# Block-decayed attention feeding an ELU MLP on one core: where the decay factors are applied, zero matmuls in the opening, and a new order of all work

## The chip, the cores and the metric

The kernel runs on one core of a Trainium2 chip. The metric is the device time of one execution in microseconds. The kernel before took 221.75 us (median of three runs, 221.27 to 222.61).

Names used below: PE is TensorE (matmuls; PEld its weight loads), DVE is VectorE, ACT is ScalarE, POOL is GpSimd, SP is SyncE. POOL issues the loads from memory (they convert float32 to float16 on the way), SP issues the DMA transposes and the stores of results.

## The reference

```python
B, H, S, D = 4, 8, 768, 64        # batch, heads, sequence, head size; blocks of 64
rel   = pos[:, None] - pos[None, :]
Dmask = where(rel >= 0, lam ** rel, 0)                 # one lam per head
for each block b:                                      # 12 blocks, in order
    intra = (qb @ kb.T * Dmask) @ vb
    inter = (qb * lam ** (pos + 1)) @ kv_state
    out_b = intra + inter
    kv_state = lam ** 64 * kv_state + (kb * lam ** (63 - pos)).T @ vb
x = out as rows of 512 (8 heads x 64), 3072 rows
h = x @ w_in                                           # 512 -> 2048
g = where(h > 0, h, exp(min(h, 0)) - 1)
result = g @ w_out                                     # 2048 -> 512, float32
```

## The kernel before

The kernel works in chunks of 128 positions instead of 64, which is possible because the decay between two positions is a product of a factor of the key and a factor of the query. There are six chunks for each of four batches, and so 24 groups: group g is chunk g // 4 of batch g % 4, with all eight heads in it. Groups g and g + 1 (g even) share one tile of x, 256 rows wide. The kernel writes its whole order by hand: ORDER is a string of tokens, and every token appends instructions to the queues of the engines, which run them strictly in that order. Two steps on different engines wait for each other only through the data and the buffers. The tokens, with what they do:

- `L:k8` loads k for groups 8 and 9 (POOL issues it; groups 0 to 3 are loaded singly, all later ones in pairs, 256 KB as float16). `i:3` and `o:3` load parts of w_in and w_out. q of group 0 alone is loaded as float32 by SP.
- `d:8` (att_kd, L275) multiplies k by its decay factors ks, on POOL (`:p`) or DVE (`:v`), giving kd.
- `t:q4` (L304) transposes q or k of one group on PE, and `e:q4` (att_T_out, L313 to L317) brings the result from PSUM to SBUF. From group 8 on, `D:k8` (att_T_dma, L297) does the same by a DMA transpose that SP issues.
- `s:8` (L328) computes the eight score tiles of a group into two PSUM banks, `E:8:0` and `E:8:1` (L335, DVE) multiply them by the mask and give pp.
- `p:8` (L349, L355) sums pp with v and, from chunk 1 on, q with the state stp, into psO; `x:8` (att_X, L372 to L376) moves psO to x.
- `u:8` (L419) computes the state's increment from kd and v, `y:8` (L402, or L396 in chunk 0; two halves on DVE) adds the old state, and `m:8` (L386, POOL) multiplies by the decay of a chunk, giving the next stp.
- `1:8:5` (L451) computes part 5 of the hidden layer for groups 8 and 9 into psH (two buffers), `h:8:5` (L461, L462, ACT) takes exp and relu, `g:8:5` (L436, DVE) joins them into g. `2:8:1` (L475) adds a quarter of the second matmul of group 8 into psM; the last quarter is followed by an ACT copy (L501) and a store. `R` (L487) does the last 128 columns of group 23.
- `z:1:0` clears a state tile, `qs:1` makes a part of the query factors qs, and `row`, `col`, `ident`, `caus`, `upp`, `ks`, `qn`, `logp` make constants. `w:3` (three matmuls of zeros) exists in the code but stands nowhere in ORDER; ten matmuls of zeros run ahead of it.

Where the decay is applied before: the key's factor is in kd, and kd is what is transposed into kT. The query's factor is applied ahead of the scores in groups 0 to 7 (by `scaled` for group 0, L263, and in the eviction of the transpose for the others, L313) and in the eviction of x from group 8 on (`GPE = 8`, L372). The mask of `E` is then only causal (`causT`, zeros and ones, the same for all heads).

BANKS names the PSUM bank of every tile: of eight banks, two hold psH and six (A, B, C, D, M0, M1) go round among transposes, scores, psO, psU and psM. The DMA transposes read kd, which has eight buffers; kT and qT have six buffers each, and the paired loads have four per tensor.

Of the kernel before, what the change touches and what calls it, by code (L numbers as in the profile page):

```python
# [15 lines left out]
def kernel(  # L16
# [11 lines left out]
    nc = tc.nc  # L28
# [11 lines left out]
    GPE = 8  # L40
# [54 lines left out]
    )  # L95
    BANKS = (
# [111 lines left out]
    qn = cpool.tile([128, H], FP32, name="qn")  # L208
# [16 lines left out]
    def const_qn():  # L225
        nc.scalar.activation(qn[:], loglam[:], AF.Exp, scale=col[:, 0:1])
# [33 lines left out]
    def scaled(w, g, eng):  # L260

        t = asb.tile([128, H, 64], FP16, tag="kd" if w == "k" else "qd", name=f"{w}d{g}", bufs=8 if w == "k" else 4)
        {"v": nc.vector, "p": nc.gpsimd}[eng].tensor_tensor(  # L263
            out=t[:], in0=raw[f"{w}{g}"][:],
            in1=(ks if w == "k" else qn)[:].unsqueeze(2).broadcast_to([128, H, 64]), op=ALU.mult,
        )
        if w == "k":
            kds[g] = t
        else:
            nat["q"][g] = t[:].unsqueeze(1)  # L270
# [23 lines left out]
    def att_T_dma(w, g):  # L294
        t = asb.tile([128, NHP, 128], FP16, tag=f"{w}T", name=f"{w}T{g}", bufs=6)
        src = of("q", g) if w == "q" else kds[g][:]
        nc.sync.dma_start_transpose(out=t[:], in_=src.rearrange("p h d -> p (h d)"))  # L297
        qkT[(w, g)] = t

    def att_T_pe(w, g):  # L300
        pt = bank(f"T{w}{g}", 0, [128, NHP, 128], FP16, f"psT{w}{g}")
        src = of("q", g) if w == "q" else kds[g][:]
        for hp in range(NHP):
            nc.tensor.transpose(  # L304
                pt[:, hp, :], in_=src[:, 2 * hp : 2 * hp + 2, :], identity=ident16[:]
            )
        psT[(w, g)] = pt

    def att_T_out(w, g, eng):
# [4 lines left out]
        elif eng == "v":  # L314
            nc.vector.tensor_copy(t[:], pt[:])
        else:
            nc.scalar.copy(out=t[:], in_=pt[:])  # L317
# [246 lines left out]
```

## Time and profile before

| | |
|---|---|
| median of three runs | 221.75 us |
| profiled execution: its own time | 222.63 us |
| profiled execution: span | 220.9 us, mean granted clock 0.959 |
| busy: PE, DVE, ACT, POOL | 206.0, 133.6, 126.6, 94.4 us |
| last matmul ends, last store lands | 217.6, 219.7 us |
| loads of q, k, v in pairs: issue to landing, median | 10.2 to 10.5 us |
| DMA transposes: issue to landing, median | 4.6 us (q), 4.8 us (k) |

The span runs from the program's first instruction to its last; what lies around it (1.7 us here) is in the execution's own time. PE's busy time is the time in which a matmul was in flight, with ends that are modelled; the clock is what the throttle granted, 1.00 being full speed. A row of the costliest groups gives line, engine, operation, tile written <- tiles read, count, busy time, mean duration of one, and the idle time of that engine just before them with what ended it.

### The profile page before, as it was taken

Reading aid. Unit: us, or ns where it says so; the run is one execution under the profiler, and the core shown is the slowest. Engines: PE = TensorE matmul, PEld = TensorE weight load, DVE = VectorE, ACT = ScalarE, POOL = GpSimd, SP = SyncE. Lnnn points to the kernel's source line nnn. Section 1 sums busy time; section 2 is a strip of 40 time slices with the busy share of each in tenths; the row PEclk is TensorE's granted clock in tenths of the full one; section 3 lists DMA queues with packets and bytes.
Section 4 is the critical chain, followed back from the end, with each engine's and each line's share of the span. In section 5 each row is a group of like instructions: output and inputs, shape, how many; then the busy total and the mean of one; then the engine's idle time right before and its main releaser. Section 6 shows DMA issues by size and latency. Waiting matters only on the chain.

```text
span 220.9 us, 4883 instructions
## 1 busy us (share of the span) xinstructions
PE 206.0 (93%) x1946; PEld 138.8 (63%) x1946; DVE 133.6 (60%) x232; ACT 126.6 (57%) x241; POOL 94.4 (43%) x113
## 2 busy tenths in 40 slices
PE   7489899999995599999999999999999999999994
PEld 2366666775763456776667676666686667676652
DVE  3787687764895457859377835487785544433230
ACT  4545666764664036656746656665665756565353
POOL 7998786968397366285942402002060000000000
PEclk9758999999999679999999999999999999999999
DMA  8999999999999999997999230502017011010115
GB/s 85 155 166 189 185 188 173 196 159 156 190 153 158 156 146 178 163 96 150 128 186 129 65 99 0 142 3 88 34 49 46 3 47 47 3 49 0 50 49 190
DMA packets 101975, 24.57 MB, mean 111 GB/s; under 512 B 92608, under 2 KB 99008, under 8 KB 101952
## 3 DMA queue, kind: packets, MB, share of 16 engines
q0 software_dynamic: 79760, 13.50, 79.3%
q1 hardware_dynamic: 22192, 10.76, 23.3%
q8 instruction: 15, 0.25, 0.4%
q14 instruction: 8, 0.07, 0.1%
HBM read 27.27 MB, written 6.29 MB: 152 GB/s over the span
## 4 chain that ended last, share of the span: by engine, by line
PE 77%; DVE 8%; DMA 5%; ACT 3%; POOL 2%; issue 1%; SPq 1%; ACTq 0%; POOLq 0%
PE psM L475 34%; PE psH L451 33%; DMA qT<-qn 4%; PE psS L328 3%; DVE pp L335 3%; PE psO L349 2%; DVE g L436 2%; PE psO L355 1%; DMA lam_b<-in_lam_dram 1%; DVE stt L402 1%; DVE stp L396 1%; PE psTk L304 1%; PE psU L419 1%; DVE qT L313 1%; POOL kd L275 1%
## 5 line engine op out<-in xcount | busy, mean ns | idle before, releaser
L436 DVE SCALAR_TENSOR_TENSOR g<-e,psH 128x512 f16<-128x512 f32 x96 | 65.7, 685 | 60.1 <-ACT psH L462 58.8
L451 PE MATMUL psH<-xt,wi 128*128 128x256 f16 x768 | 98.0, 276 | 1.4 <-ACT psH L462 1.2
L461 ACT ACTIVATE e<-psH 128x512 f32<-128x512 f32 x96 | 57.2, 596 | 64.5 <-PE psH L451 64.4
L475 PE MATMUL psM<-wo,g 128*128 128x512 f16 (+1 forms) x384 | 93.1, 382 | 0.1
L451 PEld LDWEIGHTS <-wi 128*128 128x128 f16 x768 | 74.1, 99 | 23.1 <-DVE g L436 2.0
L475 PEld LDWEIGHTS <-g 128*128 128x128 f16 x384 | 37.6, 99 | 33.6 <-issue 1.9
L462 ACT ACTIVATE psH<-psH 128x512 f32<-128x512 f32 x96 | 57.1, 595 | 0.0
L386 POOL TENSOR_TENSOR stp<-stt,upp 64x256 f16<-64x256 f32 x32 | 19.5, 609 | 59.1 <-DVE stt L402 49.5
L335 DVE TENSOR_TENSOR pp<-psS,causT 128x512 f16<-128x512 f32 x48 | 31.4, 684 | 10.9 <-PE psS L328 10.6
L501 ACT COPY osb<-psM 128x512 f32<-128x512 f32 x23 | 13.5, 586 | 17.8 <-PE psM L475 17.8
L275 POOL TENSOR_TENSOR kd<-kn,ks 128x512 f16<-128x512 f16 x18 | 18.5, 1043 | 4.1 <-issue 2.9
L159 POOL DMA_DIRECT2D kn<-in_k_dram x14 | 15.6, 1113 | 1.4 <-POOLq L548 0.8
L159 POOL DMA_DIRECT2D vn<-in_v_dram x14 | 15.3, 1096 | 2.1 <-issue 1.9
L159 POOL DMA_DIRECT2D qn<-in_q_dram x13 | 14.6, 1122 | 1.9 <-DMA qn<-in_q_dram 1.9
L328 PE MATMUL psS<-qT,kT 64*128 64x128 f16 x192 | 9.1, 237 | 6.6 <-DMA qT<-qn 4.9
L402 DVE TENSOR_TENSOR stt<-stp,psU 64x256 f32<-64x256 f16 x32 | 13.3, 414 | 0.5
L328 PEld LDWEIGHTS <-kT 64*128 64x128 f16 x192 | 6.5, 103 | 10.9 <-issue 10.2
L349 PE MATMUL psO<-pp,vn 128*64 128x128 f16 x192 | 12.8, 228 | 0.0
L372 DVE TENSOR_TENSOR xt<-psO,qs 128x512 f16<-128x512 f32 x16 | 10.8, 684 | 3.0 <-PE psO L355 2.4
L349 PEld LDWEIGHTS <-vn 128*64 128x64 f16 x192 | 10.0, 114 | 1.5 <-issue 1.4
L355 PE MATMUL psO<-qT,stp 128*64 128x128 f16 x160 | 10.6, 219 | 0.0
L355 PEld LDWEIGHTS <-stp 128*64 128x64 f16 x160 | 9.0, 110 | 0.0
(46 smaller groups left out, 74.9 us busy)
## 6 DMA issues: line engine op xcount, KB each, us to landing
out_dram<-osb SPq DMA_DIRECT2D x23, 256.0 KB, 2.2
qn<-in_q_dram POOLq DMA_DIRECT2D x10, 256.0 KB, 10.4
kn<-in_k_dram POOLq DMA_DIRECT2D x10, 256.0 KB, 10.5
vn<-in_v_dram POOLq DMA_DIRECT2D x10, 256.0 KB, 10.2
wi<-in_moe_w_in_dram POOLq DMA_DIRECT2D x8, 256.0 KB, 8.8
wo<-in_moe_w_out_dram POOLq DMA_DIRECT2D x8, 256.0 KB, 10.4
kn<-in_k_dram POOLq DMA_DIRECT2D x4, 128.0 KB, 4.9
vn<-in_v_dram POOLq DMA_DIRECT2D x4, 128.0 KB, 5.2
```

The costliest lines, as they stand in the source:

```text
L159: nc.gpsimd.dma_start(out=t[:].rearrange("p b h d -> p (b h) d"), in_=src)
L275: {"v": nc.vector, "p": nc.gpsimd}[eng].tensor_tensor(out=kd[:], in0=of("k", g), in1=ks[:].unsqueeze(2).broadcast_to([128, H, 64]), op=ALU ...
L328: nc.tensor.matmul(psS[g][hh][:, hp, :], lhsT=kt[r, hp, :], rhs=qt[r, hp, :], start=True, stop=True,)
L335: nc.vector.tensor_tensor(out=P[:], in0=psS[g][hh][:], in1=causT[:].unsqueeze(1).broadcast_to([128, NHP, 128]), op=ALU.mult,)
L349: nc.tensor.matmul(po[r, hp, :], lhsT=vt[:, 2 * hp + hh, :], rhs=Pt[(g, hh)][:, hp, :], start=True, stop=(cb == 0), skip_group_check=True,)
L355: nc.tensor.matmul(po[r, hp, :], lhsT=stp[b][cb % 2][:, hp, r], rhs=qt[:, hp, :], start=False, stop=True, skip_group_check=True,)
L386: nc.gpsimd.tensor_tensor(out=new[r, :, r], in0=stt.pop((g, hh))[r], in1=upp[r].unsqueeze(2).broadcast_to([64, NHP, 64]), op=ALU.mult,)
L436: nc.vector.scalar_tensor_tensor(out=g[:].rearrange("p f c t -> p (f c t)"), in0=e[:], scalar=-1.0, in1=r[:], op0=ALU.add, op1=ALU.min,)
L451: nc.tensor.matmul(pH[:, f * n * 128 : (f + 1) * n * 128], lhsT=wi16[i][:, kk, w * 128 : (w + 1) * 128], rhs=xg[g0][:, kk, :], start=(kk = ...
L461: nc.scalar.activation(e[:], pH[:], AF.Exp)
L462: nc.scalar.activation(pH[:], pH[:], AF.Relu)
L475: nc.tensor.matmul(psM[g][:, cols], lhsT=gts[(g, j * FB + f)], rhs=wo16[i][:, w, cols], start=first and f == 0, stop=end and f == FB - 1, ...
```

## The change

Keys and queries now go into the transposes as they were loaded, for all groups and on both ways (PE and DMA). The key's factor moves into the mask, which therefore is one tile for each head (`mask`, 128 x 1024 float32, made once on DVE), and the query's factor is applied in the eviction of x for all groups, always on DVE. kd remains for the state's increment and is no longer made for groups 20 to 23, whose state nobody reads. q of group 0 is only cast.

```diff
-    GPE = 8
-    qn = cpool.tile([128, H], FP32, name="qn")
+    mask = cpool.tile([128, H, 128], FP32, name="mask")
...
-    def const_qn():
-        nc.scalar.activation(qn[:], loglam[:], AF.Exp, scale=col[:, 0:1])
+    def const_mask():
+        nc.vector.tensor_tensor(
+            out=mask[:], in0=causT[:].unsqueeze(1).broadcast_to([128, H, 128]),
+            in1=ks[:].unsqueeze(2).broadcast_to([128, H, 128]), op=ALU.mult,
+        )
...
-    def scaled(w, g, eng):
...
+    def cast_raw(w, g, eng):
+        t = asb.tile([128, H, 64], FP16, tag=f"{w}d", name=f"{w}d{g}", bufs=4)
+        if eng == "a":
+            nc.scalar.copy(out=t[:], in_=raw[f"{w}{g}"][:])
...
     def att_T_dma(w, g):
-        src = of("q", g) if w == "q" else kds[g][:]
+        src = of(w, g)
...
     def att_T_pe(w, g):
-        src = of("q", g) if w == "q" else kds[g][:]
+        src = of(w, g)
...
     def att_T_out(w, g, eng):
-        if w == "q" and f"q{g}" not in raw:
-            nc.vector.tensor_tensor(out=t[:], in0=pt[:], in1=qs[:], op=ALU.mult)
-        elif eng == "v":
+        if eng == "v":
...
     def att_E(g, hh):
-            out=P[:], in0=psS[g][hh][:],
-            in1=causT[:].unsqueeze(1).broadcast_to([128, NHP, 128]), op=ALU.mult,
+            out=P[:], in0=psS[g][hh][:], in1=mask[:, hh::2, :], op=ALU.mult,
...
     def att_X(g):
-        if g >= GPE:
-            nc.vector.tensor_tensor(out=dst, in0=po[:], in1=qs[:], op=ALU.mult)
-        elif eng == "v":
-            nc.vector.tensor_copy(dst, po[:])
-        else:
-            nc.scalar.copy(out=dst, in_=po[:])
+        nc.vector.tensor_tensor(out=dst, in0=po[:], in1=qs[:], op=ALU.mult)
```

ORDER and BANKS are new throughout. The new ORDER holds the same steps, but for `qn` (gone), `mask` (new), `d:20` to `d:23` (gone) and four tokens of zero matmuls, `w:3`, `w:5`, `w:1` and `w:2`, eleven matmuls in all. Its opening, the stretch with the first DMA transposes, and its end:

```
L:k0 z:3:0:a L:k1 z:1:1:a i:1 log z:1:0:a iota col L:k2 row ks a:q0:a ident caus logp L:q1 t:q0 mask
upp t:k0 w:3 qs:2 e:q0:a L:v0 e:k0:a t:k1 d:0:v s:0 w:5 L:k3 d:1:v e:k1:v L:v1 E:0:1 L:q3 E:0:0 t:k2
t:q1 d:2:v L:q2 e:q1:a e:k2:v u:0 qs:1 p:0 i:0 s:1 t:k3 w:1 E:1:1 i:3 e:k3:a E:1:0 u:1 qs:0 qs:3
L:q4 p:1 x:0 t:q3 w:2 y:1 e:q3:a L:v2 x:1 s:3 t:q2 L:v3 E:3:1 1:0:1 e:q2:a z:0:1:v z:3:1:a L:k4 y:0
s:2 h:0:1 1:0:0 E:2:0 o:0 E:3:0 h:0:0 o:1 g:0:1 E:2:1 i:2 1:0:3 g:0:0 d:3:p h:0:3 u:2 p:2 t:q5 x:2
i:4 p:3 e:q5:a u:3 x:3 t:q4 o:2 e:q4:a y:3 1:2:0 o:3 g:0:3 t:k4 d:4:p h:2:0 t:k5 e:k4:v 1:2:3 d:5:p
e:k5:a s:4 g:2:0 h:2:3 s:5 E:4:0 i:5 1:2:1 z:2:1:a i:6 g:2:3 2:1:0 h:2:1 y:2 i:7 1:2:2 E:4:1 o:5
2:0:0 g:2:1 h:2:2 L:v4 1:0:2 g:2:2 L:q6 2:3:0 h:0:2 1:2:4
...
D:k8 d:9:v g:4:6 d:8:p 2:0:3 D:k9 s:7 s:6 E:7:0 1:4:7 D:q12 E:6:0 1:4:1 h:4:7 E:6:1 E:7:1 u:6 u:4
p:6 h:4:1 y:4 D:k11 p:7 m:4 g:4:7 u:7 u:5 2:3:3 y:5 D:k10 m:5 1:4:2 g:4:1 x:6 1:4:0 D:q11 h:4:2
d:10:p x:7 2:4:2 L:v10 h:4:0 g:4:2 D:q10 s:8 s:9 E:8:0 1:6:6 L:k14 g:4:0 2:4:3 h:6:6 E:8:1 D:k13
d:12:p y:7 1:4:3 g:6:6 d:13:p 2:4:0 h:4:3 D:k12 E:9:0 1:6:3 E:9:1 m:7 g:4:3 u:8 h:6:3 p:9 y:6 L:k16
u:9 p:8 y:9 s:11 D:q13 2:4:1 L:q18 E:11:0 g:6:3 1:6:5 E:11:1 1:6:2 x:8 h:6:5 2:5:1 x:9 h:6:2 g:6:5
2:5:3 z:2:0:a 1:8:4 g:6:2 m:6 d:11:v 1:6:1 h:8:4 L:v14 s:12 s:10 h:6:1 E:12:1 2:5:0
...
2:15:2 1:22:7 h:22:6 2:22:1 2:23:2 h:22:7 g:22:6 2:20:3 g:22:7 1:20:5 2:23:3 h:20:5 2:22:3 g:20:5 R
1:18:3 1:18:1 h:18:3 2:22:0 h:18:1 g:18:3 2:19:3 2:22:2 g:18:1 1:18:2 1:20:4 h:18:2 2:19:0 h:20:4
g:18:2 2:18:2 2:19:1 g:20:4 2:20:2 2:18:1 2:18:0 2:21:2
```

Before, the corresponding stretch around the DMA transposes read:

```
D:k8 E:7:1 1:4:0 E:6:0 L:k18 1:4:3 D:k9 h:4:0 E:7:0 E:6:1 u:4 L:q14 u:6 p:7 h:4:3 y:4 p:6
g:4:0 u:7 d:12:p u:5 2:2:3 y:5 m:5 D:k12 1:4:2 g:4:3 x:6:a 1:4:6 h:4:2 d:11:p x:7:v 2:3:3 d:10:p
D:k11 g:4:2 s:9 s:8 y:6 1:6:6 L:v10 h:4:6 D:k10 E:8:0 2:4:1 E:9:1 h:6:6 m:4 D:q10 g:4:6 2:4:0 g:6:6
L:q12 1:6:0 D:q11 E:9:0 1:4:4 d:13:p y:7 h:6:0 E:8:1 u:8 p:9 m:7 D:k13 h:4:4 g:6:0 u:9 p:8 1:6:5 x:8
L:k16 g:4:4 2:4:3 h:6:5 x:9 s:11 s:10
```

More of the change, by code (lines that the diff above doesn't have):

```diff
@@ L258 @@
     kds, qkT, Pt, psS, psT, psO, psU, psUU, xg = {}, {}, {}, {}, {}, {}, {}, {}, {}
-    def scaled(w, g, eng):
[L262 to L268, printed above, removed]
-        else:
-            nat["q"][g] = t[:].unsqueeze(1)
+    def cast_raw(w, g, eng):
+        t = asb.tile([128, H, 64], FP16, tag=f"{w}d", name=f"{w}d{g}", bufs=4)
+        if eng == "a":
+            nc.scalar.copy(out=t[:], in_=raw[f"{w}{g}"][:])
+        else:
+            {"v": nc.vector, "p": nc.gpsimd}[eng].tensor_copy(t[:], raw[f"{w}{g}"][:])
+        nat[w][g] = t[:].unsqueeze(1)
     def att_kd(g, eng="p"):
@@ L359, in att_P, with att_X @@
         psO[g] = po
-    def att_X(g, eng="a"):
+    def att_X(g):
         po = psO.pop(g)
@@ L507 @@
         "iota": emit_iota, "col": const_col, "row": const_row, "log": const_log,
-        "qn": const_qn, "ks": const_ks, "ident": const_ident, "caus": const_caus,
+        "mask": const_mask, "ks": const_ks, "ident": const_ident, "caus": const_caus,
         "logp": const_logp, "upp": const_upp,
@@ L519, in run @@
             x, g = a[0][0], int(a[0][1:])
-            {"L": emit_load, "a": scaled, "t": att_T_pe, "e": att_T_out}[w](x, g, *a[1:])
+            {"L": emit_load, "a": cast_raw, "t": att_T_pe, "e": att_T_out}[w](x, g, *a[1:])
         elif w == "D":
```

104 rows, old and new, of tables (BANKS, ORDER) are left out of this document.

## The prediction

> **What bounds the kernel now.** I read the page first, for the busy share and clock along the span, then three windows, PE's timeline around the hole they show, the chain of waits back from it, and SP's own waits.
>
> The page, second part (one digit is 5.5 us):
> ```profile
> PE   7489899999995599999999999999999999999994
> PEclk9758999999999679999999999999999999999999
> DMA  8999999999999999997999230502017011010115
> ```
> PE is full except in the opening and in slices 12 and 13, and both stretches have a low clock too. The DMA engines are full for the first 100 us. The windows put numbers on it (busy us of PE, PEld, DVE, ACT, POOL; then clock, DMA):
> ```profile
> 30.00:69.00 39.00, 38.86 (x438) 27.07 (x435) 29.51 (x52) 25.32 (x49) 30.02 (x32) 1.00 1.90 174
> 69.00:80.00 11.00, 6.14 (x33) 3.21 (x33) 4.77 (x9) 1.90 (x4) 4.24 (x6) 0.69 2.08 144
> 80.00:217.00 137.00, 136.84 (x1254) 92.68 (x1253) 78.81 (x131) 82.64 (x155) 33.59 (x41) 1.00 0.58 79
> ```
> From 30 to 69 and from 80 to 217 nothing but PE's own work can shorten the kernel. PE's timeline in between:
> ```profile
> 68.14 1.03 PE L475 MATMUL psM<-wo,g 128*128 128x512 f16 x4
> 74.02 1.03 PE L328 MATMUL psS<-qT,kT 64*128 64x128 f16 x16 [4.86 <-DMA qT<-qn]
> 74.99 1.89 PE L451 MATMUL psH<-xt,wi 128*128 128x256 f16 x8
> 76.67 3.49 PE L475 MATMUL psM<-wo,g 128*128 128x512 f16 x8
> ```
> s:11 waits for a DMA transpose. Four psM take 0.86 us of PE (1.73 for eight in the chain), so PE is free at 69.0 and idles 5.0 us. Then sixteen psS, eight psH and eight psM last from 74.02 to 80.17, 6.15 us, where the chain elsewhere has 0.55 + 0.87 + 1.73 = 3.15 us: 3.0 us go to a halved clock. The hole costs **8.0 us**. The chain tells why the transpose was late:
> ```profile
> 59.75 2.04 POOL kd L275 x2
> 61.80 1.16 POOL vn L159
> 62.97 0.64 POOL stp L386
> 63.61 0.44 SPq L297
> 64.14 1.32 SPq L297
> 65.51 8.37 DMA qT<-qn
> ```
> SP issues in order. D:k10 waits for kd10 on POOL, D:q10 and D:q11 stand behind it, and then the transfer needs 8.37 us in the full queue. SP's own waits (us in total, times, longest) say that it is a pattern:
> ```profile
> SPq L297 <- POOL kd L275: 19.5, 6, 5.6
> SPq L297 <- DVE stt L402: 9.3, 1, 9.3
> ```
>
> **The change, part by part.** Both programs hold the same matmuls but for eleven more zeros (w:3, w:5, w:1, w:2), so I count the time that PE loses besides its work.
>
> *Plain k into the DMA transposes.* D:k8 to D:k13 no longer wait for kd. In the new order D:q8 follows its load alone. The trace's landings give the price of a full queue: a 256 KB load every 1.67 us (48.27, 49.94, 51.60). From 47.28 to 73.89 it finished nine loads (15.0 us), nine transposes and three stores, so the latter twelve took 11.6 us, about 1.0 us each. In the new order qn8 is the 31st load; the 32nd landed at 44.36 before, so about 43.2. Up to q11 there follow two weights (1.3 each, by the landings 40.52, 41.84, 43.09), five loads, eight transposes, three stores: 10.9 + 8.2 + 2.2 = 21.3 us, hence 64.5 at best. But q11 is issued only when qn10 has landed, about 60, and issue to landing took 6.6 to 8.5 us in that stretch: 66.6 to 68.5. PE reaches s:11 after 51.7 us of work (steps of 0.87 for eight psH, 0.86 for four psM, 0.28 for eight psS), with 15.7 us lost (15.4 in the opening, below, and 0.3 in small gaps): 67.4. Idle there 0 to 1.1 us instead of 5.0. D:k13 and D:k12 wait for kn12 (about 67): k12 lands at 73 to 78, taken 75.5, and PE comes to s:12 about 74. Idle 0 to 4, taken 1.4. Later ones are due when the queue has eased: k14, behind qn16 and qn14, which POOL issues only after the state product of group 8, lands at 95 to 97, and s:14 comes at about 97: 0 to 1, taken 0. kd10 and the other kd now stand behind stp products on POOL; u:10, the first user, comes 15 us after kd10, so that costs nothing, and if POOL were that late u:10 would wait for it.
>
> *All x, and the earlier y and E, on DVE.* Between u:6 and 1:8:5 the new order gives DVE 14 E (0.684 us, L335), 20 halves of y (0.414, L402), 16 g (0.685, L436), 6 x (0.684, L372), one kd (0.683): 33.6 us, against 31 to 32 us of PE steps in the same stretch. Before, such a stretch of 24 us of PE work held 23.5 us of DVE. So DVE becomes a bound for some 32 us: up to 2.6 us, though a PE that waits for a transpose lets DVE catch up. Together with the two idles above I put **+3.0 us** (0 to 6) where 8.0 stood. A gap under 1.5 us has not dropped the clock in this trace: 1.18 us of idle at 21.7 left it at 1.00.
>
> *The opening.* Gone: q's decay and the seven qT evictions on DVE (0.676 each; now ACT copies of 0.56 to 0.59, some DVE copies of 0.42). New: the mask on DVE, 1024 wide. No row shows it; two 512-wide products (2 x 0.683) bound it above, one below; it is nearest to two, so 1.3. Walk of DVE: loglam_p done 5.8, mask 7.0, kd0 and kd1 8.4, kT1 8.8, two E 10.0, kd2 and kT2 11.1; then s:1, behind p:0 and vn0 (landed 11.01), gives E:1 at 12.2 to 13.5; x:0 waits for the last qs on ACT (13.8), then x:0, y:1, x:1 (2.2 us) to 16.0. So 1:0:1 starts at 16.1, before at 16.37. From there to g:2:2 DVE has 13.4 us in a row and waits 0.8: 30.2, and PE starts 1:2:4 at 31.05 having done 16.0 us of work. Before, 1:2:4 started at 31.72 after 16.1. The walk has the clock full; were it half until 18.5, s:1, 1:0:1 and s:2 add about 0.9. So 15.05 us lost against 15.6; the walk leaves out small gaps, and I take 15.4, **-0.2 us** (-0.6 to +1.2). The granted clock was 0.58 from 10 to 20 us although PE was busy 8.39 of 10. [...]
>
> *The end.* R moves ahead of the last psM, so the last eviction is 128x512 (0.586, was 0.266) and the last store lands in 2.0 us, not 1.76: **+0.55 us**. The dropped kd20 to kd23 cost nothing before (POOL idled 49.5 us beside them). A kn buffer is now held until its transposes land; kn16, the first load to need such a buffer, is due only at about 67, ten us after they do.
>
> Sum: span 220.9 - 8.0 + 3.0 - 0.2 + 0.55 = 216.3. The profiled execution took 222.63, 1.73 more than its span: 218.0. It lay 0.9 above the median of 221.75, so **217.1 us**. The likeliest case's own range is 215 to 219.
>
> **Rivals.** *No hole at all*: queue and DVE keep up, residue 0: 214.1. For it: the queue's bare work ends at 64.5. Against: 33.6 us of DVE.
> *One idle long enough to halve the clock*: k12 lands at 77 or later; 3 us more, as after 74.02: 220.1. For it: kT13 took 8.19 us before.
> *Slower*: the clock drops twice, at s:11 and at s:12, because loads and transposes share the queue: each time 2 us of idle and 3 us of half clock, 10 us for the 3.0: 224.1. It decides from idles of about 1.8 us each: the clock here changes at steps of 3.41 us (4.81, 8.22, 18.46, 73.08, 79.91), it stayed full with 1.18 us of idle, and it fell at 8.22 after a step in which PE worked about half the time. For it: the DMA column is nearly as high from 30 to 69 (1.90) as in the hole (2.08). Against: SP would have to issue q11 2 us later than I have it.
> [...]
>
> **How the numbers follow.** Forecast 0.50 (0.15 of it with the half clock in the opening), no hole 0.18, one dropped clock 0.19, two 0.13. The range 213.9 to 222.0 leaves out the double drop and the best edge. 0.5% (1.1 us), about what a measurement can tell, puts the limits at 220.6 and 222.9: faster 0.50 + 0.18 + 0.11 = 0.79, same 0.09, slower 0.12.
>
> **What would show it.** Right: PE's digits near 9 in slices 11 to 14; SP's waits on POOL's kd gone; no wait of psS for a DMA over 2 us; DVE near 10 of 10 from 56 to 88; PE's last matmul at about 212.5. Wrong: a psS wait of over 3 us with PEclk below 1 behind it, or 1:2:4 later than 33.

## The result, and the profile after

The changed kernel takes 226.97 us (median of four runs, 225.91 to 228.12), beside 221.99 us for the kernel before: a ratio of 1.0239 with a 95% interval of 1.0206 to 1.0272. It is 2.4% slower where 2% faster was forecast. Here and below, ratios leave out executions more than 1.5% above the fastest of their kernel, while medians and ranges hold all of them. Its profiled execution took 225.91 us with a span of 224.1 us and a mean clock of 0.977, against 222.63, 220.9 and 0.959 before.

The second part of the page of the changed kernel:

```profile
PE   7787999999997999954999999999999999999992
PEclk9969999999999999996799999999999999999999
DMA  8999999999999999999999675010120001101114
```

Counted from 0, the hole of slices 12 and 13 is gone but for a 7 in slice 12. There is a new one in slices 17 and 18, and it too has a low clock at its end (slices 18 and 19). The windows of the changed kernel size both (busy us of PE, PEld, DVE, ACT, POOL; then clock, DMA):

```profile
60.00:69.50 9.50, 7.87 (x108) 5.51 (x106) 8.14 (x16) 5.09 (x10) 4.28 (x5) 1.00 1.78 159
69.50:98.00 28.50, 27.89 (x296) 19.54 (x296) 21.94 (x38) 16.43 (x32) 24.20 (x29) 1.00 1.75 140
98.00:109.00 11.00, 4.93 (x32) 2.72 (x31) 2.57 (x4) 2.17 (x5) 4.64 (x5) 0.69 2.09 186
```

The last line is nearly a copy of the line from 69 to 80 us of the kernel before (clock 0.69, DMA 2.08): the hole has not been closed but moved 29 us later. PE's timeline of the changed kernel shows who waits there; the bracket is the idle time ahead and what ended it:

```profile
69.50 0.40 PE L324 MATMUL psS<-qT,kT 64*128 64x128 f16 x8 [1.63 <-DMA qT<-qn]
...
104.18 1.04 PE L324 MATMUL psS<-qT,kT 64*128 64x128 f16 x16 [6.07 <-DMA kT<-kn]
105.15 1.89 PE L465 MATMUL psM<-wo,g 128*128 128x512 f16 x4
106.83 1.91 PE L441 MATMUL psH<-xt,wi 128*128 128x256 f16 x8
108.54 2.07 PE L465 MATMUL psM<-wo,g 128*128 128x512 f16 x8
110.45 1.04 PE L441 MATMUL psH<-xt,wi 128*128 128x256 f16 x8
```

s:11 waits 1.6 us, s:12 (76.02) not at all, and s:14 waits 6.1 us for the transpose of k14. Behind it eight psH take 1.91 us where they take 1.04 at 110.45, which is the halved clock (granted 0.50 from 102.04 to 108.87). The chain of waits leads one step further back:

```profile
94.82 1.29 SPq L295
...
96.20 7.93 DMA kT<-kn
104.14 0.05 issue
104.18 1.04 PE psS L324 x16
```

k14 was issued late, at 96.2 us, and then took 7.9 us. SP's row and POOL's row of the same stretch stand side by side in the changed kernel:

```profile
89.60 2.50 SPq L295 DMA_TRANSPOSE qT<-qn  x2
92.19 1.22 SPq L295 DMA_TRANSPOSE kT<-kn  x1
93.52 2.59 SPq L295 DMA_TRANSPOSE qT<-qn  x2
96.20 2.72 SPq L295 DMA_TRANSPOSE kT<-kn  x2
```
```profile
93.61 1.21 POOL L158 DMA_DIRECT2D vn<-in_v_dram  x1
94.81 1.17 POOL L158 DMA_DIRECT2D kn<-in_k_dram  x1
95.95 1.17 POOL L158 DMA_DIRECT2D vn<-in_v_dram  x1
97.08 1.18 POOL L158 DMA_DIRECT2D qn<-in_q_dram  x1
```

SP's row q16, q17, k17, q15, q14, k14 starts when qn16 lands (89.55), and every transpose takes SP 1.3 us. POOL issues four loads at the same time (v22, k18, v18, q20, for groups of which the first, s:18, is due on PE at 133.8 us): v22 stands 1.2 us ahead of q14, three of the four ahead of k14, and q20 0.9 us behind it. The trace's landings: k17, issued at 92.19, took 2.51 us, q14 6.97 and k14 7.93. The balance of the span (+3.2 us): the hole at s:11 gone -8.0, s:11 now +1.8, a gap inside p:12 +0.9, s:14 with its halved clock +8.5, the end +0.6, and -0.6 in the opening and small gaps.

### The profile page after: what moved, and what is told of

The parts are those of the page before. It is cut to its first block, busy times and chain, and to the rows that moved or that the text cites. A ratio compares the mean times of both kernels' runs of the same rounds, so it can differ in the third digit from the quotient of the medians.

```text
span 224.1 us, 4888 instructions
## 1 busy us (share of the span) xinstructions
PE 207.3 (92%) x1957; PEld 138.2 (62%) x1957; DVE 133.9 (60%) x231; ACT 128.1 (57%) x243; POOL 89.5 (40%) x108
## 4 chain that ended last, share of the span: by engine, by line
PE 78%; DMA 9%; DVE 5%; POOL 2%; issue 2%; ACT 1%; SPq 1%; POOLq 0%; ACTq 0%
PE psH L441 35%; PE psM L465 34%; DMA kT<-kn 4%; DMA qT<-qn 3%; PE psS L324 3%; PE psO L344 2%; DMA vn<-in_v_dram 2%; DVE pp L331 2%; PE psO L350 2%; DVE g L426 1%; POOL kn L158 1%; PE psU L409 1%; SPq L295 1%; DVE xt L366 1%; ACT e L451 1%
## 5 line engine op out<-in xcount | busy, mean ns | idle before, releaser
L465 PE MATMUL psM<-wo,g 128*128 128x512 f16 (+1 forms) x384 | 93.6, 380 | 0.0
L331 DVE TENSOR_TENSOR pp<-psS,mask 128x512 f16<-128x512 f32 x48 | 31.6, 685 | 13.0 <-PE psS L324 12.7
L273 POOL TENSOR_TENSOR kd<-kn,ks 128x512 f16<-128x512 f16 x13 | 13.4, 1038 | 12.8 <-DMA kn<-in_k_dram 8.6
L366 DVE TENSOR_TENSOR xt<-psO,qs 128x512 f16<-128x512 f32 x24 | 16.1, 686 | 1.9 <-PE psO L350 0.9
L324 PEld LDWEIGHTS <-kT 64*128 64x128 f16 x192 | 6.0, 99 | 12.1 <-DMA kT<-kn 6.6
L120 PE MATMUL psZ<-zero 128*128 128x512 f16 x21 | 8.0, 528 | 1.2 <-DVE zero L115 1.2
```

What stands on the lines that cost most here:

```text
L324: nc.tensor.matmul(psS[g][hh][:, hp, :], lhsT=kt[r, hp, :], rhs=qt[r, hp, :], start=True, stop=True,)
L331: nc.vector.tensor_tensor(out=P[:], in0=psS[g][hh][:], in1=mask[:, hh::2, :], op=ALU.mult,)
L366: nc.vector.tensor_tensor(out=dst, in0=po[:], in1=qs[:], op=ALU.mult)
L465: nc.tensor.matmul(psM[g][:, cols], lhsT=gts[(g, j * FB + f)], rhs=wo16[i][:, w, cols], start=first and f == 0, stop=end and f == FB - 1, ...
```

## The experiments

The theory: the change did close the hole it aimed at, and the new order opened another, because q14 and k14 are issued (a) late and (b) among four loads that nobody needs yet. The rivals: (a) alone, (b) alone, DVE as the bound, and the move of the decay itself. Ratios are against the kernel before on the same chip.

**The four loads held back (e1).** A copy on POOL that reads the masked scores of group 17 stands ahead of them:

```diff
+    def gate(g, hh):
+        nc.gpsimd.tensor_copy(gate_sb[:], Pt[(g, hh)][:, 0, 0:8])
 ORDER
-  1:8:7 L:v22 h:8:2 D:k15 2:6:1 L:k18 h:8:7 g:8:2 2:7:1 L:v18 1:8:0 g:8:7 1:8:3 L:q20 h:8:0 s:14
-  s:17 d:16:p h:8:3 g:8:0 2:6:3 E:17:1
+  1:8:7 h:8:2 D:k15 2:6:1 h:8:7 g:8:2 2:7:1 1:8:0 g:8:7 1:8:3 h:8:0 s:14
+  s:17 d:16:p h:8:3 g:8:0 2:6:3 E:17:1 G:17:1 L:k18 L:v22 L:v18 L:q20
```

> The changed kernel with the four loads v22, k18, v18, q20 held back on POOL until s:17 is done (a copy of 8 columns of its masked scores stands ahead of them). Theory 'crowded queue': these four loads, issued at 93.6 to 97.1 us, are what made the transpose k14 take 7.9 us. Without them q14 (issued about 94.8) and k14 (about 96.2) land in 2.5 to 3.5 us, k14 at 98.7 to 99.7; PE is ready for s:14 at 98.1, so the hole of 6.1 us shrinks to 0.6 to 1.6 us, the clock stays full behind it, and of the 8.5 us lost there about 7 to 7.9 come back: 219 to 220 us. Rival 'late issue': the transposes take as long as they do because k14 comes at the end of nine transposes issued in a row; then k14 still lands at 102 or later, and the time stays at 225 or above.

Measured: 223.68 us, ratio 1.0092 (1.0060 to 1.0124). k14 was issued at 96.67, no earlier than in the first profile of the changed kernel, and landed after 2.48 us. PE's timeline of this kernel:

```profile
97.23 1.91 PE L441 MATMUL psH<-xt,wi 128*128 128x256 f16 x16
99.19 0.62 PE L324 MATMUL psS<-qT,kT 64*128 64x128 f16 x16
...
113.73 0.40 PE L324 MATMUL psS<-qT,kT 64*128 64x128 f16 x8
117.37 0.40 PE L324 MATMUL psS<-qT,kT 64*128 64x128 f16 x8 [3.24 <-DMA kT<-kn]
```

s:14 follows psH without a wait, so the crowding is shown: the same transpose, issued within 0.5 us of the same time, lands after 2.5 us without the four loads and after 7.9 with them. Loads that POOL issues thus delay a transpose that SP issues, by 5.4 us in this pair of runs. The time of 219 to 220 us was missed because the wait was passed on: SP's next transposes k19 and k18 wait for the late load k18, and k16 behind them landed at 117.3, so s:16 waited 3.2 us and the clock halved again.

**The same, with k16 ahead (e1b).**

```diff
-  ... D:k15 ... D:k19 d:18:p 2:9:1 L:k22 g:8:1 D:k18 ... D:k16
+  ... D:k15 ... D:k16 D:k19 d:18:p 2:9:1 L:k22 g:8:1 D:k18 ...
```

> The changed kernel with the four late loads, and D:k16 moved ahead of D:k19 and D:k18 on SP. In the run with the late loads alone k14 landed at 99.2 us after 2.5 us and s:14 did not wait, but SP then stood at D:k19 for the load kn18 (issued at 101.5, landed at 106.2), D:k16 behind it landed at 117.3, and s:16 waited 3.4 us and lost 0.8 more to a halved clock. Theory 'the wait was passed on': k16, whose load landed long before, is issued behind k15 at about 99 and lands by 102; s:16 does not wait; 4.2 us come back: 219 to 220 us. Rival 'the queue is full there whatever the order': s:16, s:18 or an eviction waits instead, 222 us or more.

Measured: 218.71 us, ratio 0.9859 (0.9816 to 0.9902), with a granted clock of 1.00 in the whole profiled execution. PE's timeline around s:14 and s:17:

```profile
97.16 1.91 PE L441 MATMUL psH<-xt,wi 128*128 128x256 f16 x16
99.68 0.62 PE L324 MATMUL psS<-qT,kT 64*128 64x128 f16 x16 [0.61 <-DMA kT<-kn]
```

The time lies just below the 219 to 220 expected. Two edits to the order of DMA issues bring back 8.3 us of the changed kernel's 226.97 (9.3 us of the 228.02 that it takes on this chip, c0 below) and put it 1.4% below the kernel before. The wait of 0.6 us that remains at s:14 is the lateness (a) by itself.

**The two query loads early (e2).** This removes (a) and leaves the four loads where they are:

```diff
-  L:q18 ... L:v14 ... d:17:p ... m:9 ... m:8 ... L:q16 ... L:v16 ... L:q14
+  L:q18 L:q16 L:q14 ... L:v14 ... d:17:p ... m:9 ... m:8 ... L:v16
```

> The changed kernel with the loads q16 and q14 right behind q18 on POOL, ahead of v14, kd17 and the state products of groups 9 and 8; nothing else moved. Theory 'late issue': k14 is issued only at 96.2 us because SP's row q16 q17 k17 q15 q14 k14 starts with the landing of qn16 at 89.55. With qn16 landing near 84 the row starts behind q19 (84.2) and k14 is issued near 90.5, ahead of the four loads, and lands by 95: no wait at s:14, clock full, 218 to 219 us. Rival 'crowded queue alone': the two loads only move the crowd 8 us forward, k12, k14 or v14 land later in it, a hole of 3 us or more opens at s:12, s:13 or s:14, and the time stays above 222 us.

Measured: 219.59 us, ratio 0.9879 (0.9843 to 0.9916). The time lies just outside the 218 to 219 expected. k14 was issued at 94.06, not near 90.5 as expected, since qn18 at the head of SP's row landed 2.5 us later than in the first profile; but the four loads followed only at 96.37. In SP's and POOL's rows of this kernel:

```profile
94.06 2.53 SPq L295 DMA_TRANSPOSE kT<-kn  x2
```
```profile
96.37 1.21 POOL L158 DMA_DIRECT2D vn<-in_v_dram  x1
```

k14 landed after 2.61 us, and s:14 did not wait. So either edit is enough for s:14: what counts is which of the two rows, SP's or POOL's, comes to that point first. The load ahead of the four, v16, had landed at 93.98, so the queue held no load when k14 was issued.

**The changed kernel again (c0).**

> The changed kernel as it is, on the chip and beside the runs of the two kernels that follow, to see how far k14's landing moves from one execution to the next: in its first profile kn16 landed at 78.6 us and k14 at 104.1, while with the zeros in the gap they landed at 81.7 and 107.7, though both programs are the same up to there. Theory 'the queue drifts': kn16 lands at 79 to 82 here, k14 at 104 to 108, and each microsecond of it is in the hole at s:14; time 226 to 228 us. Rival 'the zeros in the gap push the loads back': kn16 at 78.6 and k14 at 104.1 again.

Measured: 228.02 us, ratio 1.0269 (1.0218 to 1.0321). kn16 landed at 80.6, k14 was issued at 98.54 and landed at 106.66, and s:14 waited 7.4 us:

```profile
106.71 1.04 PE L324 MATMUL psS<-qT,kT 64*128 64x128 f16 x16 [7.43 <-DMA kT<-kn]
```

The same program lands its loads 2 to 3 us earlier or later from one profiled execution to the next, and the hole carries it into the time. The record does not say whether the first profile was taken on this chip. Four programs that are the same up to there (c0, e1, e1b, e6), on two chips, have kn16 at 80.6 to 81.7, so it is the first profile's 78.6 that stands apart.

**Zeros in the gap (e6).**

```diff
-  1:8:3 L:q20 h:8:0 s:14 s:17 d:16:p h:8:3 g:8:0
+  1:8:3 L:q20 h:8:0 g:8:0 w:20 s:14 s:17 d:16:p h:8:3
```

> The changed kernel with twenty matmuls of zeros (4.3 us of PE) ahead of s:14, where PE idled 6.1 us; g:8:0 is put ahead of them so that their bank is free. Theory 'idle halves the clock': the zeros fill most of the gap, the clock stays full after 102 us, s:14 starts as before near 104.2, and the 2.4 us that s:14, s:17, 2:6:3 and 1:8:1 lost behind it come back: 224 to 224.8 us. Rival 'the clock falls for another reason than idleness' (for one, the transfers): half clock behind s:14 as before, 226.5 to 227.5 us.

Measured: 226.81 us, ratio 1.0210 (1.0167 to 1.0254), so the time says no gain. PE's timeline says what happened:

```profile
101.38 4.48 PE L120 MATMUL psZ<-zero 128*128 128x512 f16 x20 [1.08 <-DVE g L426]
107.72 0.62 PE L324 MATMUL psS<-qT,kT 64*128 64x128 f16 x16 [1.86 <-DMA kT<-kn]
108.27 1.04 PE L465 MATMUL psM<-wo,g 128*128 128x512 f16 x4
109.15 1.04 PE L441 MATMUL psH<-xt,wi 128*128 128x256 f16 x8
```

The clock stayed full: eight psH take 1.04 us behind s:14, not 1.91, and from s:14 to the last matmul it is 113.8 us, against 116.0 and 116.5 in the two traces without these zeros. So idleness halved the clock, for some 2.2 to 2.7 us. But k14 landed at 107.7 here, 1 us later than in c0, and that ate it. The forecast of 224 to 224.8 had taken the first profile's 104.2 for granted.

**The decay alone, in the old order (e4).** ORDER and BANKS of the kernel before; `mask` behind `caus`, `qn` and `d:20` to `d:23` left out, x always on DVE.

> The order and banks of the kernel before, with the decay where the change puts it: mask on DVE behind the causal mask, q and k plain, x always times qs on DVE; the four kd that only fed transposes and the new zeros are left out. Theory 'two causes': the decay by itself frees D:k10 of kd10, but q11 stands behind qn10, which landed at 63.3 us in the kernel before, so q11 is issued at about 64.7 instead of 65.5 and the hole at s:11 keeps 3 to 5 us of idle and its half clock; x and the mask on DVE add 0.5 to 1 us in the opening: 221 to 223 us. Rival 'the decay alone removes the hole': 214 to 216 us. Second rival 'the decay alone costs' (DVE becomes the bound): 224 or more.

Measured: 222.32 us, ratio 1.0010 (0.9974 to 1.0045). The windows, which answer to those of the kernel before:

```profile
30.00:69.00 39.00, 38.78 (x437) 26.95 (x435) 29.71 (x54) 24.77 (x46) 29.10 (x32) 1.00 1.93 173
69.00:80.00 11.00, 8.64 (x114) 6.05 (x113) 8.00 (x14) 3.99 (x8) 5.79 (x7) 1.00 2.47 139
80.00:215.00 135.00, 133.10 (x1180) 89.31 (x1178) 76.54 (x127) 80.91 (x152) 30.27 (x37) 1.00 0.63 80
```

q11 landed at 72.1 instead of 73.9, and PE came 1.4 us later out of the opening, so s:11 waited 1.6 us in this execution and the clock held. The times of this kernel spread from 220.75 to 223.93. From 80 to 215 us PE idles 1.9 us, where the kernel before idles 0.2 from 80 to 217. On the median the decay by itself neither gains nor costs: what made the changed kernel slower came with the new order.

**Without the zeros (e5).** e2 with `w:3`, `w:5`, `w:1` and `w:2` taken out.

> The kernel with q16 and q14 early (219.59 us, profile 220.3) without the eleven zeros of w:3, w:5, w:1, w:2. Theory 'the landing of q11 covers the opening': q11 is issued when qn10 has landed, about 62.5 us, and lands at about 70.1 whatever PE did before; PE stood ready at 67.5 and waited 2.6 us. Without the zeros the clock is half in part of the opening and PE comes 0.5 to 2 us later, but the wait at s:11 shrinks by the same: 219 to 220.5 us. Rival 'zeros pay in full': 1 us or more slower, 220.7 or above. Second rival 'the clock holds by itself': granted clock of 1.0 through the opening without them, and PE at s:8 at the same time as with them.

Measured: 217.80 us, ratio 0.9832 (0.9791 to 0.9873). The opening did become worse: s:8 started at 63.13 instead of 61.28. But s:11 started at 69.57, no later than with zeros (70.25), because q11 landed at 68.95. The landing covers the opening, as expected, though the time came out below the 219 to 220.5 given. The rest of the difference between the two profiles lies in a gap of some 2 us inside p:12 in e2, which is missing here; the profile puts 1.52 us of it to "issue", and its cause is open. The intervals of e2 and e5 overlap, so it is shown that the zeros gained nothing there, and not that they cost.

**Loads and transposes of groups 10 to 13 by need (e7).** On e2:

```diff
-  L:q12 ... L:q10 ... D:q12 ... D:k11 ... D:k10 ... D:q11 ... L:v10 ... D:q10 ... L:k14 ... D:k13 d:12:p ... d:13:p ... D:k12 ... D:q13
+  L:q10 ... L:q12 ... D:q11 ... D:k11 ... D:k10 ... D:q10 ... D:q12 D:q13 ... D:k12 d:12:p ... d:13:p L:v10 L:k14 ... D:k13
```

> The kernel with q16 and q14 early, and the loads and transposes of groups 10 to 13 in the order of their need: qn10 takes the place of qn12 among the loads and qn12 that of qn10; SP's row becomes q11, k11, k10, q10, q12, q13, k12, k13; the loads v10 and k14 go behind kd12 and kd13 on POOL. Theory 'landings set PE from 67 to 78': q11 lands at about 62, s:11 does not wait (2.6 us back), k12 lands at 73 to 75 with two loads less ahead of it and s:12 does not wait (0.9 us): 215.5 to 217 us. Rival 'DVE is the bound there' (33.6 us of its work against 31 to 32 us of PE steps, as the prediction had it): the waits for transposes go, waits for DVE's g and E take their place, 218 to 219.5 us. Second rival: v10 or k14 is late now, and u:10 or s:14 waits, 219 or more.

Measured: 221.11 us (four executions, 217.96 to 222.41), ratio 0.9897 (0.9803 to 0.9990, on the two that are left). The 215.5 to 217 expected was missed. s:11 started at 67.64 and s:12 at 74.31, both without a wait. A wait that none of the theories had named took their place, by the table of waits from 60 to 90 us:

```profile
PE psO L350 <- POOL stp L376: 3.1, 3, 2.2
```

On POOL five loads and kd17 (which waits for kn16, landed at 82.07) stand ahead of the state products of groups 9 and 8, as in e2, and p:13 and p:12 need them; PE came there some 3 us earlier than in e2.

**POOL's row by need as well (e8), and the same without zeros (e9).** On e7, behind `d:13`: `L:v10 m:7 L:q18 m:6 L:k16 m:9 L:q16 m:8 L:q14 L:k14 L:v14 d:17`.

> The kernel with loads and transposes of groups 10 to 13 by need (221.11 us, profile 220.9), with POOL's row behind kd13 put by need too: v10, product 7, q18, product 6, k16, product 9, q16, product 8, q14, k14, v14, kd17. In the run before it, s:11 and s:12 no longer waited, but kd17 and five loads stood ahead of the products of groups 9 and 8, p:13 and p:12 waited for stp on POOL 3.0 and 1.4 us, and the halved clock behind cost 1.2 more. Theory 'POOL's row was the rest of it': these 5.7 us come back, k14 is issued behind SP's row at about 94 and lands by 97: 215 to 216.5 us. Rival 'DVE bounds the stretch anyway': waits for g, E or x in their place, 218 or more. Second rival: k14's load, now issued at about 83, lands after 93 and s:14 waits: 219 or more.

> The same without the eleven zeros of w:3, w:5, w:1, w:2. Theory 'what covers the opening is gone': with the zeros out the clock is half for part of the opening and PE came to t:q4 1.9 us later in the earlier run; there the wait at s:11 took it up, here s:11 does not wait (q11 lands at about 62), so it costs 1 to 2 us against the kernel with zeros: 216 to 218 us. Rival 'zeros never pay' (the loads set the whole stretch up to 85 us even so): equal to or faster than the kernel with zeros.

Measured: 221.21 us, ratio 0.9937 (0.9910 to 0.9965), and 218.78 us, ratio 0.9832 (0.9804 to 0.9860). Both theories missed. In e8 (its profiled execution took 223.6 us, 2.4 more than its median, so it is read for the order and not the size) PE waited for no landing longer than 0.4 us between 60 us and s:14, but came there earlier, at 96.8, and k14 had been issued at 95.53, behind the first late load at 94.96 and with v16, landed at 97.64, still under way: it took 7.09 us. In e9 k14 was ahead of the late loads by 1.0 us and landed at 98.46. That the kernel without zeros is the faster one is the opposite of what was expected; whether the zeros had a part in where the two rows met is not shown.

**All by need (e10), and without zeros (e11).** On e8: the load of q14 changes places with q18's, k14's goes ahead of q16's and k16's; SP's row is q14, k14, q17, k17, q15, k15, q16, k16, q18, q19; kd17 goes behind product 11; the four loads behind the gate of e1.

> All of it by need: the order of the run before (s:11, s:12 and p:13 no longer waited, PE stood ready for s:14 at 96.8 us, but k14 landed at 102.6), plus the loads q14, k14, q16, k16 ahead of q18, SP's row as q14, k14, q17, k17, q15, k15, q16, k16, q18, q19, kd17 behind product 11, and the four late loads held back until s:17 is done. Theory 'only the order of the queue is at fault, it has room for all of it': k14 is issued before 90 us and lands by 96, s:14 does not wait, the 6.0 us of wait and 1.6 us of half clock come back: 213 to 215 us, what the prediction had for 'no hole at all' (214.1). Rival 'the queue's total work is the bound': the bytes ahead of k17 and k14 are the same, s:14, s:17 or s:15 waits, 217 or more. Second rival 'DVE': 216 to 218 with waits for g and E.

> The same without the eleven zeros of w:3, w:5, w:1, w:2. Without any wait for a landing between the opening and s:14, what the opening costs is seen in full: by the two traces of the runs before, PE with zeros came to s:14 some 0.7 us earlier than without. Theory 'zeros pay once nothing covers them': 0.5 to 1.5 us slower than the kernel with zeros. Rival 'zeros never pay': equal or faster.

Measured: 215.70 us, ratio 0.9712 (0.9677 to 0.9748), and 216.29 us, ratio 0.9742 (0.9715 to 0.9769). e10 is the best version of the study, just above the 213 to 215 expected, 2.9% below the kernel before and 11 us below the changed one, with the same matmuls. Its page and windows:

```profile
PE   7875999999999979999999999999999999999992
PEclk9999999999999999999999999999999999999999
DMA  7999999999999499999999992101110001101124
```
```profile
60.00:69.50 9.50, 9.46 (x121) 6.56 (x122) 8.87 (x17) 5.38 (x10) 1.10 (x2) 1.00 1.75 162
69.50:98.00 28.50, 27.38 (x302) 19.21 (x301) 21.41 (x39) 17.19 (x33) 24.50 (x29) 1.00 1.69 143
98.00:109.00 11.00, 11.00 (x72) 6.89 (x72) 6.20 (x9) 6.66 (x13) 8.08 (x8) 1.00 1.53 144
```

k14 was issued at 83.2 and took 6.8 us in the full queue, but landed at 90.0, and s:14 started at 97.34 right behind psH. One wait is left, 1.1 us of u:10 for vn10. With and without zeros differ by 0.6 us in the direction expected, with intervals that overlap: not settled.

The landings of k14 in all traces of the new order, one row for each profiled execution (us; the issue of the first of the four late loads, the issue of k14, its time to landing, its landing, and PE's idle time at s:14):

| kernel | late loads | k14 issued | took | landed | idle at s:14 |
|---|---|---|---|---|---|
| changed | 93.6 | 96.2 | 7.9 | 104.1 | 6.1 |
| changed again (c0) | 94.8 | 98.5 | 8.1 | 106.7 | 7.4 |
| e6 | 95.8 | 99.3 | 8.4 | 107.7 | 1.9, behind the zeros |
| e8 | 95.0 | 95.5 | 7.1 | 102.6 | 5.9 |
| e9 | 93.4 | 92.4 | 6.1 | 98.5 | 1.1 |
| e5 | 94.8 | 93.8 | 2.5 | 96.3 | 0 |
| e2 | 96.4 | 94.1 | 2.6 | 96.7 | 0 |
| e7 | 96.7 | 95.0 | 2.5 | 97.5 | 0 |
| e1 | 101.5 | 96.7 | 2.5 | 99.2 | 0 |
| e1b | 101.7 | 97.2 | 2.5 | 99.6 | 0.6 |
| e10 | 99.7 | 83.2 | 6.8 | 90.0 | 0 |
| e11 | 99.7 | 82.7 | 6.2 | 88.9 | 0 |

Where no 256 KB load was under way when k14 was issued (e5, e2, e7, e1, e1b) it landed after 2.5 to 2.6 us, even with the four loads 1.0 to 2.3 us behind it. Where one or more were, it took 6.1 to 8.4. In e9 it was ahead of the four, but two others (v14 and v16, landed at 94.4 and 97.4) were still in the queue.

## Why the prediction was wrong

**The hole at s:11: right.** It was to go, and it went. SP's waits of the changed kernel no longer hold kd; the transposes wait for loads (us in total, times, longest):

```profile
SPq L295 <- DMA qn<-in_q_dram: 55.2, 4, 42.5
SPq L295 <- DMA kn<-in_k_dram: 21.0, 6, 7.2
```

q11 was issued at 61.74 (about 60 was said) and landed at 69.36, just beyond the 66.6 to 68.5 given; s:11 lost 1.8 us. k12 landed at 75.87 (75.5 was said), and s:12 lost nothing. With the gap in p:12 the residue is 2.7 us for the +3.0 forecast, but that the sums agree is in part luck: the forecast had 1.4 us at s:12, which measured 0, and a share for DVE, which was not needed, and it had no gap in p:12.

**The opening and the end: right.** 1:2:4 started at 31.52 (31.05 was said), so the opening gained 0.1 us where 0.2 was said. The full clock of its walk was the author's assumption: no trace had shown it, and the clock granted from 10 to 20 us was 0.83. The mask took 1.22 us for the 1.3 taken. The end cost 0.6 us for 0.55.

**The step that failed** is the sentence on the later transposes: "Later ones are due when the queue has eased: k14, behind qn16 and qn14 ..., lands at 95 to 97, and s:14 comes at about 97: 0 to 1, taken 0." PE was ready for s:14 at about 98. k14 landed at 104.1, and the term taken as 0 measured 8.5 us: 6.2 of wait and 2.3 of halved clock. Two things were left out of it. First, SP's row: six transposes stand ahead of and with k14 behind the landing of qn16, 1.3 us apart, so that k14 is issued at 96 to 98 however empty the queue. e1b prices this at 0.6 us. Second, the queue had not eased: POOL's next four loads were in the new ORDER between D:k14 and s:14, and nothing held POOL back from issuing them while SP still worked through its row. e1 prices this at 5.4 us of landing time. The price of such crowding stood in the prediction's own rows (6.6 to 8.5 us from issue to landing in the full stretch) and was used for q11 but not for k14; for k14 an eased queue was taken. The DMA 0.58 from 80 to 217 us suggests it, but that is a mean over a stretch of which most is quiet. In the page's DMA row the kernel before has nines, but for a 7 in slice 18, up to slice 21, which ends at 121 us, and its windows around the time of k14 (the DMA column is the last but one) read:

```profile
90.00:100.00 10.00, 10.00 (x114) 7.34 (x112) 6.71 (x13) 6.16 (x13) 5.46 (x6) 1.00 1.34 138
100.00:110.00 10.00, 10.00 (x72) 6.87 (x71) 6.11 (x12) 7.01 (x15) 7.98 (x10) 1.00 1.00 133
```

Then follows 2.15 from 110 to 120. In the new order the column reads 2.09 from 98 to 109. The sign of being wrong that the prediction named, a psS wait of over 3 us with a low clock behind it, came at s:14.

**DVE as the bound: wrong.** Up to 2.6 us were set aside for it. e10 has the same DVE work and ran from 60 to 109 us with PE idle for little beside u:10's wait, no DVE wait among it. DVE was busy 8.87 of 9.5 us at most.

**The rivals.** "No hole at all", 214.1 us, was not what this ORDER does, but e10 reached 215.7 with the same work, so the queue has the room. "One idle long enough to halve the clock" was put at s:12, where k12 came in time. "The clock drops twice because loads and transposes share the queue", priced at 10 us, named the right mechanism (e1: 5.4 us of landing time) at the wrong place: it was put at s:11 and s:12, and happened once, at s:14, for 8.5 us. The half clock in the opening, to which 0.15 of the forecast was given, lasted 3.41 us of the changed kernel (13.29 to 16.71; 10.24 before). With the zeros the granted clock from 10 to 20 us was 0.83 in the changed kernel and 1.00 in e10, and without them in e11 it was 0.50:

```profile
10.00:20.00 10.00, 8.41 (x86) 5.69 (x86) 6.44 (x14) 4.64 (x10) 9.94 (x12) 0.50 2.17 168
```

e10 has 7.08 us busy there. That e11 is busy for longer may come from the half clock alone, since the same matmuls take longer at half the clock (eight psH 1.91 us at 106.83 in the changed kernel and 1.04 at 110.45). The stretches of half clock last 6.83 us behind s:14 in the changed kernel, 10.24 in c0 and 3.41 each time in e1 (twice).

## What to carry to other kernels

When a new order brings a step forward, follow its operands back through every queue that they share: the issuing engine's row (here 1.3 us for each transpose ahead of it) and the transfers that another engine may issue at the same moment. A wait that disappears on one engine lets its successors run ahead (in e7 PE came to p:13 some 3 us earlier than in e2), and a load that is issued early for its own sake can make an urgent transfer three times as long (k14: 7.9 us, and 2.5 without the four loads); hold such loads back with a data dependence, or order both rows by when each landing is needed. Price the step at the crowded rate unless the row shows that it comes first, and where two rows meet within 2 or 3 us, divide most of the chance between both outcomes.

## What the runs showed that was not expected

- Two rows of issues that meet within about 2.5 us decide over 5 us: a transpose of 128 x 512 issued 1.0 to 2.3 us ahead of the four loads into a queue without other loads took 2.5 to 2.6 us (e5, e7, e2), and one issued behind the first of them 7.9 to 8.4 (changed kernel, c0, e6).
- The landings of one and the same program moved by 2 to 3 us between its two profiled executions (kn16 at 78.6 and 80.6, k14 at 104.1 and 106.7), in a stretch where its opening differs by 0.3 us.
- The length of an idle time alone did not decide the clock. At s:11, 2.6 us (e2) and 2.2 us (e1b) left it at 1.00, but 2.2 us in e1 halved it, for 3.41 us from 70.08, and so did gaps of 2.2, 0.4 and 0.4 us close together in e7. What separates them is PE's busy time in each step of 3.41 us (between its changes the clock held for 10.24, 54.61 and 6.83 us in the kernel before and for 3.41, 85.33 and 6.83 in the changed one, all multiples of 3.41), counted back from the changes of the clock (where there is none, from the start of its record): 1.22 us in e1 (66.67 to 70.08) and 1.12 in e7 (82.52 to 85.93), but 1.61 in e1b (67.68 to 71.09) and 1.87 in e2 (65.81 to 69.22). In all these traces, from 60 us on and at full clock, each of the seven steps with 1.23 us or less was followed by half clock and none with 1.61 or more. The steps begin at another point in each trace (the record of the clock starts at 3.8 to 7.0 us), so in these runs one and the same idle time of about 2 us cost half clock in one execution and nothing in another. The 1.8 us of the prediction's third rival, an estimate that fits one step of the kernel before (3.41 less 1.59 busy, 4.81 to 8.22), is no limit in these runs.
- A worse opening cost nothing as long as a landing set the next step: 1.85 us later at s:8, but not later at s:11 (e5).
